# Ten more groups of spare products among the scores and state products of the first units, in a fused HGRN2 and FNet kernel

## The chip, the cores and the metric

The kernel runs on one core of one Trainium2 chip. The metric is device time in microseconds: 553.58, the median of 5 runs (553.43 to 553.75). TensorE (PE) multiplies and transposes, VectorE (DVE) and ScalarE (ACT) do the elementwise work, GpSimd (POOL) helps, and nearly all loads are issued from SyncE's queue (SP).

## What is computed

Two blocks follow each other. The first is a linear recurrence with a gate for each channel, over 4 batches, 8 heads, 768 tokens and 48 channels:

```python
f = 1.0 / (1.0 + np.exp(-f_logit))
for t in range(S):
    state = f[:, :, t, :, None] * state + np.einsum('bhd,bhe->bhde', k[:, :, t], v[:, :, t])
    y[:, :, t] = np.einsum('bhd,bhde->bhe', q[:, :, t], state)
```

The heads are then put side by side (384 columns), and the second block is an FNet mixer: u is x plus the real part of a two-dimensional FFT over tokens and columns; then u is normalized, multiplied by w_ch1 (384 x 1536), passed through a ReLU, multiplied by w_ch2 (1536 x 384) and added to u. Everything is in fp32; the weights arrive in double words and are converted in the kernel.

## The kernel before

**Units.** The recurrence is cut into 16 units of two heads of one batch (four units a batch). A unit is a Python generator, `attention`, that goes on in `outputs`; each call runs it to its next `yield`. Its steps, with the line numbers of the profile:

1. ACT: exp and ln of the gate (L330, L331).
2. DVE: the running sum of the gate's logarithm as a scan into W (L337), and chunk ends into `deep` (L338; POOL L339).
3. ACT: the exponentials (L342, L343, L345).
4. DVE: q and k are scaled in place (L349, L350).
5. PE: the **scores**, 24 small products in two halves (L361, `sc`).
6. DVE: the scores are masked into `at` (L368), one instruction for each half.
7. PE: five transposes of the scaled k (L506, `st`), and ACT copies them out (L508, `kT`).
8. PE: the **state products** k times v for each chunk (L517, `ds`).
9. DVE: the scan over chunk states (L525, `stt`).
10. PE: y within the chunks (L537).
11. PE: y from the earlier states, added to the same banks (L544); ACT: five copies to `yT` (L553 to L557).
12. PE: transposes of `yT` (L564, `yt`); ACT: copy into x (L566).
13. POOL and DVE: `fold`, sums and differences of x for the Fourier stage (L590 to L612).

The tiles `sc`, `st`, `ds` and `yt` share a PSUM pool of two buffers (`ps_a`), so each waits until the one before the last has been read.

**Behind the units.** For each batch `fnet` does the Fourier products (L650 `z`, L669 `mix`) and the normalization, whose rows are turned by PE (L708, `pt`). `projected` does the two big products (L750 `up`, L759 `po`, L773 `fx` and `fz`). Meanwhile the weights are converted block by block: ACT L238, DVE L240 and L241, POOL L242, each from one of three `raw` buffers.

**The order is written out by hand.** `ORDER` is one string of 676 words, and the loop at the end of the function runs one step for each word, in this order on every engine. A number is a step of that unit. L5qv loads q and v of unit 5 (f, k, q and v stand for the gate, k, q and v); r fetches a raw weight block and C converts one; F and H are steps of the Fourier stage, P of the projections. **D calls `busy` (L150)**:

```python
for _ in range(4):
    nc.tensor.matmul(spare, lhsT=bound[:, :C], rhs=bound[:, :2 * C], start=not started, stop=True,
                     skip_group_check=True)
    started.append(True)
```

A D is thus four products of 128 x 128 by 128 x 256 in bf16 on a constant tile, into 256 columns that nothing reads (L153). `spare` lies in the same PSUM tile as y, behind y's 768 columns, so a spare product can wait for ACT's copies of y. Before the change there are 21 such words, 84 products: 16 words in the first 13.7 us, three behind the scores of unit 3, and one behind the transposes of unit 4 and one before those of unit 5.

**Loads.** SP issues its DMAs in order, and each waits for the eighth before it. The load of a unit's q waits until PE has done L544 for the unit that used the same buffer (four buffers for q, three each for k and the gate).

Of the kernel before, what the change touches and what calls it, by code (L numbers as in the profile page):

```python
# [12 lines left out]
C = 128  # L13
# [12 lines left out]

ORDER = (
    "Gq2 r I D Gq0 L0f Gk1 L1f D Gk0 L0q i D Gq3 C Gq1 Z L0k 0 D 1 Gk2 0 L1q 1 L1k D D D D D D D D D D D "
    "D 0 0 1 0 r 1 L2f 0 2 C L1v 1 L3fk 1 3 L0v 0 1 L2q 2 0 0 r 1 L2k 3 1 0 2 r 3 L3q 2 L2v 0 C L3v C "
    "L4fk R 4 2 2 3 1 0 C 2 4 1 3 L5qv D L4qv L5fk 3 D D 3 2 0 2 3 2 3 C r 4 1 4 L6fk C r 2 5 4 L6qv 4 2 "  # L30
    "1 5 6 3 4 D 4 C 5 3 T 3 6 4 5 5 4 2 r L7fk 7 5 D L7qv 3 5 S L8fk C 4 7 6 6 5 F0 5 r r F0 F0 F0 7 4 "
    "C F0 L9fk 5 6 8 H0 H0 6 5 6 r H0 C L8qv 6 7 L9qv P0 6 7 r C P0 7 7 C 9 P0 r r 5 8 C r C F0 r 7 F0 6 "
    "P0 5 9 C 6 7 P0 r C P0 8 8 C P0 r r 7 P0 P0 8 9 H0 C P0 P0 8 7 8 C P0 H0 7 9 6 H0 H0 C 9 r C P0 9 "
    "L10fk r 9 P0 r C 9 L11fk 10 C 6 P0 11 4 P0 P0 P0 P0 P0 P0 10 P0 P0 P0 L10qv P0 P0 7 F1 9 P0 F1 H0 9 "
    "W P0 P0 P0 11 F1 P0 L11qv P0 P0 P0 9 P0 P0 P0 8 L12fk P0 11 11 8 P0 P0 10 11 F1 P0 11 11 10 L14fk "
    "F1 8 P0 14 F1 P0 10 P0 8 10 P0 P0 H1 H1 10 L12qv P0 P0 10 P0 F1 P0 11 11 10 P0 10 H1 P0 P0 P0 P0 12 "
    "12 12 P0 P0 12 P0 H1 P0 12 P0 H1 L13fk P1 P1 P1 P1 P1 14 13 P1 12 8 8 P1 P1 12 9 10 L13qv 13 P1 P1 "
    "L14qv 9 P1 12 11 P1 H1 11 10 P1 P1 13 P1 13 P1 12 P1 P1 14 P1 14 V 13 P1 c V 10 P1 P1 P1 P1 P1 V "
    "L15fk P1 13 P1 11 V P1 P1 P1 P1 c P1 11 F2 V c F2 F2 H1 13 H1 F2 c 14 P1 c V c P1 P1 12 P1 P1 14 P1 "
    "P1 13 V V V P1 15 F2 c P1 12 P1 P1 P1 P1 c P1 H2 14 15 V V P1 P1 P1 P1 P1 13 P1 14 F2 P1 c P1 P1 15 "  # L40
    "V 13 P1 H2 P1 P1 L15qv P1 14 13 P1 V 12 H2 F2 14 P2 P2 P2 P2 P2 P2 P2 15 P2 P2 P2 c c 12 H2 V H2 15 "
    "H2 15 P2 c P2 15 P2 P2 15 P2 14 13 15 P2 P2 14 P2 P2 15 13 P2 P2 P2 P2 P2 H2 V 15 P2 P2 14 15 H2 P2 "
    "P2 P2 P2 15 F3 F3 P2 F3 F3 P2 F3 c P2 P2 P2 P2 P2 V P2 c P2 V c c V P2 P2 P2 P2 P2 c P2 F3 F3 P2 V "
    "P2 H3 P2 P2 P2 H3 H3 P2 P2 P2 P2 P2 P2 P2 P2 P2 P2 P3 H3 c P3 P3 P3 P3 V P3 c P3 P3 P3 c V V c P3 "
    "P3 P3 H3 P3 P3 P3 P3 P3 P3 c P3 P3 V P3 H3 P3 P3 P3 P3 P3 P3 H3 H3 P3 P3 P3 P3 P3 P3 P3 P3 P3 P3 P3 "
    "P3 V P3 P3 P3 P3 P3 c P3 c P3 P3 P3 M P3 P3 P3 P3 P3 P3 P3 P3 P3 P3 P3 P3"
)

PAIRS = ((0, 3), (2, 5), (1, 4))
# [925 lines left out]
```

## Time and profile before

| | us |
|---|---|
| median of 5 runs | 553.58 (553.43 to 553.75) |
| the profiled execution | 554.17 |
| its span, from the first to the last instruction | 552.4 |
| PE busy | 525.4 (95%) |
| DVE busy | 299.7 (54%) |
| ACT busy | 192.6 (35%) |
| POOL busy | 94.4 (17%) |
| L153, the spare products | 84 of 0.27 each (median, pipelined) |

The profile is of one execution. Its rows are instructions with start and length, and consecutive ones of the same line are merged; `[1.34 <-DVE at L368]` says that the engine was idle for 1.34 us before the first of them and that DVE's L368 on tile `at` ended this. PEclk is the share of TensorE's clock that was granted. PE's products are pipelined: the length of one (0.27 us) is longer than the distance between two starts. A product in fp32 appears as two records.

### The profile page before, as it was taken

The numbers are of one execution on the slowest core, as the hardware profiler recorded it, in microseconds if no ns is written. First come the engines' busy times: TensorE is split into PE (matmuls) and PEld (weight loads), VectorE is DVE, ScalarE is ACT, GpSimd is POOL, SyncE is SP. The second block draws the span as 40 slices with busy tenths as digits, with TensorE's granted clock in tenths as the row PEclk, the third lists the DMA queues.
The fourth block names the chain that finished last, engine by engine and source line by source line (L and its number), as shares of the span: only waits on it lengthen the run. The fifth ranks groups of instructions, "written<-read, shape, count | busy, mean of one in ns | idle before, by whom it ended". The sixth has DMA issues, their size and how long they took to land.

```text
span 552.4 us, 10204 instructions
## 1 busy us (share of the span) xinstructions
PE 525.4 (95%) x4186; PEld 461.2 (83%) x4186; DVE 299.7 (54%) x534; ACT 192.6 (35%) x497; POOL 94.4 (17%) x147
## 2 busy tenths in 40 slices
PE   7787699999999999999999999999999999999995
PEld 5676578876898889889889899899889798989985
DVE  8899899984936527435744444453452342413231
ACT  5768286672332333441340422321411303021110
POOL 7146535534101000130201001003001000010000
PEclk9799799999999999999999999999999999999998
DMA  8989645463302100412530301102003004000001
GB/s 203 235 246 230 191 135 166 118 187 94 76 0 72 36 9 2 116 44 78 166 115 15 115 1 58 30 1 87 0 30 87 1 8 165 0 30 0 30 2 34
DMA packets 18398, 44.38 MB, mean 80 GB/s; under 512 B 3109, under 2 KB 4710, under 8 KB 18342
## 3 DMA queue, kind: packets, MB, share of 16 engines
q1 hardware_dynamic: 17094, 39.89, 26.6%
q0 software_dynamic: 1104, 3.54, 1.8%
q8 instruction: 35, 0.57, 0.5%
q10 hardware_dynamic: 144, 0.20, 0.1%
q14 instruction: 21, 0.17, 0.1%
HBM read 38.90 MB, written 4.72 MB: 79 GB/s over the span
## 4 chain that ended last, share of the span: by engine, by line
PE 86%; DMA 5%; ACT 3%; DVE 2%; POOL 1%; issue 1%; SPq 1%; ACTq 0%; POOLq 0%
PE up L750 34%; PE fx L773 16%; PE fz L773 12%; PE z L650 3%; PE y L537 3%; DMA g<-in_qkf_dram 3%; PE y L544 3%; PE sc L361 3%; PE po L759 3%; PE mix L669 3%; PE ds L517 2%; PE yt L564 1%; PE pt L708 1%; PE st L506 1%; DMA tab<-in_seq_tab_dram 1%; DMA q<-in_qkf_dram 1%
## 5 line engine op out<-in xcount | busy, mean ns | idle before, releaser
L750 PE MATMUL up<-unT,w 128*128 128x256 f32 x864 | 197.0, 382 | 1.5 <-DVE x L728 0.9
L750 PEld LDWEIGHTS up<-unT,w 128*128 128x128 f32 x864 | 161.0, 190 | 26.1 <-issue 1.5
L752 ACT ACTIVATE h<-up 128x256 f32<-128x256 f32 x144 | 55.2, 383 | 199.2 <-PE up L750 199.2
L617 POOL DMA_INDIRECT out_dram<-x,place x16 | 16.9, 1057 | 270.7 <-DVE x L803 232.6
L773 PE MATMUL fx<-block,h 128*128 128x192 f32 x264 | 46.5, 326 | 0.0
L773 PE MATMUL fx<-w,h 128*128 128x192 f32 x264 | 44.9, 327 | 0.1
L773 PEld LDWEIGHTS fx<-w,h 128*128 128x128 f32 x264 | 43.1, 190 | 0.8 <-ACT h L752 0.4
L773 PEld LDWEIGHTS fx<-block,h 128*128 128x128 f32 x264 | 43.5, 190 | 0.0
L242 POOL TENSOR_TENSOR w<-w,raw 128x384 uint32<-128x384 uint32 x24 | 29.7, 1244 | 47.8 <-ACT raw L238 24.0
L780 DVE TENSOR_TENSOR s<-h,h 128x768 f32<-128x768 f32 x11 | 10.5, 954 | 50.4 <-ACT h L752 50.4
L361 PE MATMUL sc<-q,W 48*64 48x128 f32 x768 | 26.4, 283 | 7.4 <-issue 4.4
L361 PEld LDWEIGHTS sc<-q,W 48*64 48x64 f32 x768 | 22.0, 138 | 11.6 <-issue 6.9
L368 DVE COPY_PREDICATED at<-causal,sc 128x768 f32<-128x768 uint32 x32 | 31.2, 1032 | 0.8 <-PE sc L361 0.8
L337 DVE TENSOR_TENSOR_SCAN W<-g,bound 112x768 f32<-112x768 f32 x16 | 29.5, 1843 | 1.0 <-issue 0.5
L725 DVE TENSOR_TENSOR x<-mix,x 128x384 f32<-128x384 f32 x12 | 6.6, 553 | 38.6 <-PE mix L669 38.6
L537 PE MATMUL y<-at,v 128*64 128x128 f32 (+1 forms) x384 | 26.2, 287 | 0.0
L537 PEld LDWEIGHTS y<-at,v 128*64 128x64 f32 (+1 forms) x384 | 22.6, 137 | 3.1 <-issue 2.9
L773 PE MATMUL fz<-w,s 128*128 128x192 f32 x132 | 23.5, 328 | 0.0
L773 PE MATMUL fz<-block,h 128*128 128x192 f32 x132 | 23.5, 328 | 0.0
L773 PE MATMUL fz<-w,h 128*128 128x192 f32 x132 | 23.4, 327 | 0.0
L695 ACT ACTIVATE rstd<-mv,eps 128x1 f32<-128x1 f32 (+1 forms) x20 | 5.9, 294 | 46.0 <-DVE mv L692 46.0
L773 PEld LDWEIGHTS fz<-w,s 128*128 128x128 f32 x132 | 21.6, 190 | 0.3 <-issue 0.3
(145 smaller groups left out, 743.3 us busy)
## 6 DMA issues: line engine op xcount, KB each, us to landing
raw<-in_w_ch_dram SPq DMA_DIRECT2D x24, 384.0 KB, 4.8
g<-in_qkf_dram SPq DMA_DIRECT2D x32, 144.0 KB, 4.6
q<-in_qkf_dram SPq DMA_DIRECT2D x32, 144.0 KB, 4.6
k<-in_qkf_dram SPq DMA_DIRECT2D x32, 144.0 KB, 5.4
v<-in_v_dram SPq DMA_DIRECT2D x16, 288.0 KB, 4.9
k<-in_w_ch_dram SPq DMA_DIRECT2D x12, 384.0 KB, 4.0
g<-in_w_ch_dram SPq DMA_DIRECT2D x12, 384.0 KB, 4.3
out_dram<-x SPq DMA_DIRECT2D x4, 168.0 KB, 2.1
```

Source lines behind the costliest of these rows:

```text
L242: nc.gpsimd.tensor_tensor(bits, bits, lo, ALU.add)
L337: nc.vector.tensor_tensor_scan(W, g, bound[:R], 0.0, ALU.add, ALU.min)
L361: nc.tensor.matmul(ps[64 * s:64 * s + 64, r, i * C:(i + 1) * C], lhsT=W[ROWS[r], o + 64 * s:o + 64 * s + 64], rhs=Q[ROWS[r], o:o + C], sta ...
L368: nc.vector.copy_predicated(AT[:, :, half], causal.bitcast(U32).unsqueeze(1).unsqueeze(1).to_broadcast([128, 2, NCH // 2, C]), ps[:, :, :N ...
L537: nc.tensor.matmul(y[FILL[r], c * C:(c + 1) * C], lhsT=vt[:, c, r * D:r * D + (64 if r == 0 else D)], rhs=AT[:, r, c], start=(c % 4 == 0), ...
L544: nc.tensor.matmul(y[ROWS[r], c * C:(c + 1) * C], lhsT=st[ROWS[r], :, c - 1], rhs=Q[ROWS[r], c * C:(c + 1) * C], start=False, stop=True, s ...
L617: nc.gpsimd.indirect_dma_start(out=out.rearrange("b s d -> (b s) d"), out_offset=bass.IndirectOffsetOnAxis(ap=place[:, b, i:i + 1], axis=0 ...
L650: nc.tensor.matmul(z[:, cols], lhsT=src[:, j, lo:hi], rhs=tab[:, t, T % 2, cols], start=(i == 0), stop=(i == len(parts) - 1), skip_group_c ...
L669: nc.tensor.matmul(mix[:, o], lhsT=zz[:rows_of[T], T, PLACES[c]], rhs=cd[:rows_of[T], T, :NQ - odd], start=(i == 0), stop=(i == 1))
L750: nc.tensor.matmul(pp[:, :256], lhsT=w1[:, kt, m * 128:(m + 1) * 128], rhs=unT[:, kt], start=(kt == 0), stop=(kt == 2))
L752: nc.scalar.activation(hs[-1][:, m % H].rearrange("p t n -> p (t n)"), pp[:, :256], AF.Relu)
L773: nc.tensor.matmul(out, lhsT=h[:, m], rhs=blocks[i][:, m], start=(start and m == 0), stop=(m == H - 1), skip_group_check=True)
```

## The change

Ten more words D stand in `ORDER`, in four places; nothing else differs. The words around them, with the new ones as `+D`:

```
D 0 0 1 0 +D +D +D r 1 L2f 0 2 C L1v 1 +D +D L3fk 1 3 L0v 0 1
L5qv D L4qv L5fk 3 D D +D +D +D 3 2 0 2 3 2 3 C r 4 1 +D +D 4 L6fk C r 2 5 4
```

On PE the 40 new products come to stand

- (a) 12 between the scores of unit 0 and the scores of unit 1,
- (b) 8 between the scores of unit 1 and the transposes of unit 0,
- (c) 12 behind the scores of unit 3 and the 12 spares that stand there already, ahead of the transposes of unit 3,
- (d) 8 between the transposes of `yT` of unit 1 and L544 of unit 2.

The core of the diff (the string is wrapped anew behind each place):

```diff
-    "D 0 0 1 0 r 1 L2f 0 2 C L1v 1 L3fk 1 3 L0v 0 1 L2q 2 0 0 r 1 L2k 3 1 0 2 r 3 L3q 2 L2v 0 C L3v C "
-    "L4fk R 4 2 2 3 1 0 C 2 4 1 3 L5qv D L4qv L5fk 3 D D 3 2 0 2 3 2 3 C r 4 1 4 L6fk C r 2 5 4 L6qv 4 2 "
+    "D 0 0 1 0 D D D r 1 L2f 0 2 C L1v 1 D D L3fk 1 3 L0v 0 1 L2q 2 0 0 r 1 L2k 3 1 0 2 r 3 L3q 2 L2v 0 "
+    "C L3v C L4fk R 4 2 2 3 1 0 C 2 4 1 3 L5qv D L4qv L5fk 3 D D D D D 3 2 0 2 3 2 3 C r 4 1 D D 4 L6fk "
```

## Prediction

> **What bounds the kernel now.** I read the page's slices first, then the busy times on a grid of short stretches, then the timelines of TensorE (PE) and VectorE (DVE) around the four places.
>
> ```profile
> PE   7787699999999999999999999999999999999995
> DVE  8899899984936527435744444453452342413231
> PEclk9799799999999999999999999999999999999998
> ```
>
> From the seventh slice on (13.8 us each) PE is full, and in 85 to 548 us it is busy for 459.29 of 463.00 us. Whatever is gained or lost before about 85 us is carried unchanged to the end. Before that PE has gaps, DVE is the full engine, and the granted clock dips twice.
>
> The clock moves on a grid. One-microsecond stretches give a mean clock of 0.74 in 19:20 and 0.85 in 26:27, so it was halved from 19.48 to 26.30 us; 0.51 in 57:58 and 0.58 in 63:64 give 57.02 to 63.84. These are steps of 6.82, 30.72 and 6.82 us, all multiples of 3.41. So I asked for stretches of that length (start:end, length, busy us and instructions of PE, PEld, DVE, ACT, POOL, then the clock):
>
> ```profile
> 16.06:19.48 3.42, 1.79 (x49) 1.30 (x49) 3.39 (x6) 2.93 (x6) 0.88 (x1) 1.00 1.02 218
> 19.48:22.89 3.41, 2.63 (x21) 2.22 (x23) 2.79 (x3) 2.42 (x6) 0.33 (x2) 0.50 1.07 252
> 22.89:26.30 3.41, 3.41 (x52) 3.41 (x50) 2.43 (x3) 2.04 (x3) 0.00 (x0) 0.50 1.03 242
> 43.37:46.78 3.41, 1.94 (x52) 1.75 (x54) 3.29 (x4) 3.29 (x10) 1.61 (x1) 1.00 1.02 242
> 53.61:57.02 3.41, 1.09 (x12) 0.66 (x8) 3.38 (x4) 2.52 (x8) 1.94 (x5) 1.00 0.80 209
> ```
>
> The clock fell after PE was busy for 1.79 and 1.09 us, and did not fall after 1.94 us. The sign of a fall is a stretch about half empty.
>
> ```profile
> 16.76 1.81 PE L361 MATMUL sc<-q,W 48*64 48x128 f32 x48 [1.34 <-DVE at L368]
> 19.46 2.13 PE L506 MATMUL st<-ident,W 112*128 112x112 f32 x10 [0.89 <-DVE at L368]
> 22.38 2.42 PE L517 MATMUL ds<-v,kT 128*64 128x48 f32 x39 [0.78 <-ACT kT L508]
> ```
>
> This is PE in the first dip. The state products (ds) took 2.42 us; the same 39 at full clock take 1.40 (at 39.69, below).
>
> **Parts (a) and (b): 12 spares between the scores of units 0 and 1, 8 between the scores of unit 1 and the transposes of unit 0.** A spare costs 0.109 us on PE: twelve took 1.47 us from first start to last end with a pipeline tail of 0.27 (the row at 36.99 below), so (1.47-0.27)/11. Twelve cost 1.31 and eight 0.87 at full clock, about double at half clock (an estimate from the 2.42 against 1.40 of ds, which is 1.7). The scores of unit 0 issue until 15.26 (13.88+1.54-0.27+0.11) and those of unit 1 wait until 16.76 for DVE's L368: 1.31 fits into that 1.50. The scores of unit 1 issue until 18.41 and the transposes wait until 19.46, again for L368: 0.87 fits into 1.05. So both cost nothing while L368 is late; if that cover were gone they would cost 2.18.
>
> What they buy: stretch 16.06:19.48 rises from 1.79 busy to about 1.79+0.5+0.87 = 3.1, far above the 1.94 that kept its clock. So the fall at 19.48 goes. The transposes then end earlier, but ds starts at 22.38 as before, since its v arrives only then (SP's queue records the landing of that v at 22.24). With ds at full clock its first half ends after 0.85 (row at 68.19, x20) instead of some 1.4, so DVE's state scan, 23.84 before, starts about 0.54 earlier. This carries to the scores of unit 2 (28.94, right after DVE's L350).
>
> **Is it kept?** Not on DVE:
>
> ```profile
> 34.31 0.36 DVE L240 TENSOR_SCALAR w<-raw 128x384 uint32<-128x384 uint32 x1 [0.16 <-DMA raw<-in_w_ch_dram]
> ...
> 40.47 0.36 DVE L593 TENSOR_TENSOR eo<-eo 128x192 f32<-128x192 f32 x1
> 40.74 1.40 DVE L525 TENSOR_TENSOR_SCAN stt<-ds,te 112x288 f32<-112x288 f32 x2
> 42.06 0.34 DVE L240 TENSOR_SCALAR w<-raw 128x384 uint32<-128x384 uint32 x1
> 42.44 0.84 DVE L241 SCALAR_TENSOR_TENSOR w<-raw,w 128x384 uint32<-128x384 uint32 x1
> ```
>
> At 34.31 DVE waits for a weight block that was issued at 28.40 from a stream that fills the DMA engines (share about 1.0 from 5 to 34 us), so arriving 0.54 earlier only lengthens that wait. From 34.31 on DVE is busy back to back up to the second `pt` transposes, apart from 1.49 us at 60.49 that wait for POOL, which itself waits for DVE:
>
> ```profile
> 80.77 0.52 PE L708 MATMUL pt<-ident,un 128*128 128x128 f32 x3 [0.17 <-PE sc L361]
> ...
> 83.57 0.55 PE L708 MATMUL pt<-ident,un 128*128 128x128 f32 x3 [0.38 <-DVE un L705]
> ```
>
> PE waits for DVE at 83.57 and hardly again. So the time is what DVE's chain from 34.31 to 83.51 makes it. Parts (a) and (b): 0 (bounds -0.54 and 0).
>
> **Part (c): 12 more spares behind the 12 already there, ahead of the transposes of unit 3.**
>
> ```profile
> 36.99 1.47 PE L153 MATMUL y<-bound 128*128 128x256 bf16 x12
> 38.77 0.70 PE L506 MATMUL st<-ident,W 112*128 112x112 f32 x5 [0.31 <-DVE at L368]
> 39.69 1.40 PE L517 MATMUL ds<-v,kT 128*64 128x48 f32 x39 [0.22 <-DVE at L368]
> ```
>
> Here the cover is 0.31 us and the new work 1.31. The last of 24 spares starts at 36.99+23x0.109 = 39.50, the transposes at 39.61 instead of 38.77 (+0.84). They end at 40.31, and the kT copy on ACT (0.63, at 39.50 before) ends at 40.97. The ds of unit 2 follow the transposes at 40.13, end at 40.98, and DVE's first scan starts at 41.02 instead of 40.74 (+0.28, since L593 ends at 40.83). The ds of unit 3 wait for kT, run 41.02 to 41.87, and the second scan starts at 41.90 instead of 41.41: **+0.49 on DVE**, the engine without slack. Part comes back: L241 at 42.44 took 0.84 against 0.56 at 34.71, while POOL's L596 ran until 42.86; 0.49 later it starts after that and takes 0.56. That leaves **+0.21**. Behind it POOL's L242 (1.61 at 43.41) and DVE's L350 (1.76 against 0.95 at 33.19) obstruct each other as before, both 0.21 later. Bounds: 0 if ds is quicker, +0.49 if nothing comes back.
>
> **Part (d): 8 spares ahead of the inter-chunk products of unit 2 (L544, 43.13).** +0.87 and the delay of (c) put their end near 46.0 instead of 44.47. PE was then idle until 45.94, when the scores of unit 4 wait for DVE's L350, itself 0.21 later: hidden, with about 0.2 to spare. ACT's copies of y2 move from 44.51 to 46.0; ACT was idle from 47.27 to 48.87 before. SP's q load for unit 6 waits for L544 and goes from 45.49 to about 46.0; the load behind it starts at 47.26. Cost 0; without this cover up to 0.87.
>
> The order of instructions on DVE, ACT, POOL and SP does not change. **Sum:** 0 + 0 + 0.21 + 0 = +0.21 us. The profiled execution took 554.17 us around its span of 552.4; the median of the five runs is 553.58. I apply the difference to the median: 553.8.
>
> The Trainium skill, page "TensorE: Matmul & The Clock Gate", Part 1, says that the clock halves after at least one idle window of about 3.4 us on a free-running grid. The row 16.06:19.48 agrees in the length but not in "idle": PE was busy for 1.79 of 3.42 us. By the page's wording nothing would fall there and (a) and (b) would buy nothing; by the row they buy 0.54, which DVE then loses. Either way the sum is +0.21. The page's free-running grid speaks against spares at fixed places, since another execution could have other windows; no run here shows that, and five runs lie within 0.32 us.
>
> **Rivals.**
> 1. *The clock falls later instead (slower).* With ds and y0 at full clock, PE reaches the end of unit 0's L544 at about 26.5 instead of 28.25, and still waits for DVE until 28.40. Stretch 26.30:29.72, 2.74 busy before, would hold about 0.2 + 1.3 = 1.5, less than the 1.79 that fell. Then 29.72:33.13 runs at half clock and loses 1.71; unit 1's L544 ends at 33.93+1.71 = 35.64 instead of 34.49, and with it the q load on SP. The chain of waits runs from exactly there (SP, q, g, table, g until 65.8, ACT, z at 72.22): +1.15, 554.7; with a second half-clock stretch +2.86, 556.4. It decides when that stretch is emptier than about 1.8. For: the numbers above. Against: stretch 19.48:22.89 (about 1.9 busy with everything at full clock) may fall first, as a rest of the old dip up to 26.30; then the change barely does what it says, and the time is my forecast's.
> 2. *The DMA chain binds, not DVE.* The chain of waits goes from L544 at 34.49 through SP and DMA; 0.54 earlier there gives 553.0. For: the page's chain. Against: DVE without gaps beside it.
> 3. *DVE and POOL fall differently.* The scan at 52.69 took 3.24 against 1.75 elsewhere while POOL did 1.5 us of work; this can vanish (-1.49+0.21, 552.3) or arise at another scan, such as 49.95 (+1.7, 555.3).
>
> **Chances.** Forecast, 553.4 to 554.1: 0.55. Rival 1: 0.16, of which 0.12 is slower by over 0.2% (1.1 us, about what a measurement of this kernel can tell from no change). Rival 2: 0.14. Rival 3: 0.15, of which 0.08 faster and 0.07 slower. So faster 0.08, same 0.73, slower 0.19. The range 552.6 to 554.9 takes in the bounds of (a) to (d), rival 2 and rival 1's first price; it leaves out rival 3's ends and rival 1's second price.
>
> **What the new profile would show.** Right: clock 1.00 in 19.48:22.89; the waits before the transposes at 19.46 unchanged; DVE still waiting at 34.3; the ds of unit 3 and the second scan near 41.9; `pt` at 83.8. Rival 1: a clock of 0.50 in 29.72:33.13. I am wrong if DVE's wait at 34.31 goes, if scans change by over 1 us, or if PE at 83.57 no longer waits for DVE.

## The result: slower by 0.32%

The changed kernel took **555.93 us** (median of 42 executions) against 554.14 for the kernel before (median of 73 on the same chips): a ratio of **1.0032, interval 1.0022 to 1.0042**, or 1.8 us (1.2 to 2.3). Two executions of the changed kernel, at 690.6 and 691.2 us with a mean granted clock of 0.75, were disturbed and are left out of the ratio. The prediction was 553.8 with a range of 552.6 to 554.9, and 0.73 for "within 0.2%": wrong. The kernel before also shows that five executions had been too few: 73 of them lie between 552.7 and 557.9.

### The profile page after: what moved, and what is told of

It is laid out like the page before. It is cut to its first block, busy times and chain, and to the rows that moved or that the text cites. A ratio compares the mean times of both kernels' runs of the same rounds, so it can differ in the third digit from the quotient of the medians.

```text
span 552.8 us, 10284 instructions
## 1 busy us (share of the span) xinstructions
PE 527.8 (95%) x4226; PEld 463.5 (84%) x4226; DVE 299.4 (54%) x534; ACT 192.5 (35%) x497; POOL 94.5 (17%) x147
## 3 DMA queue, kind: packets, MB, share of 16 engines
q0 software_dynamic: 1104, 3.54, 1.9%
## 4 chain that ended last, share of the span: by engine, by line
PE 85%; DMA 6%; ACT 3%; DVE 3%; issue 1%; POOL 1%; SPq 0%; ACTq 0%; DVEq 0%; POOLq 0%
PE up L750 34%; PE fx L773 15%; PE fz L773 12%; PE z L650 3%; PE y L537 3%; PE sc L361 3%; PE po L759 3%; PE mix L669 3%; PE y L544 3%; DMA raw<-in_w_ch_dram 2%; DMA g<-in_qkf_dram 2%; PE ds L517 2%; PE yt L564 1%; PE pt L708 1%; DMA tab<-in_seq_tab_dram 1%; PE st L506 1%
## 5 line engine op out<-in xcount | busy, mean ns | idle before, releaser
L617 POOL DMA_INDIRECT out_dram<-x,place x16 | 16.9, 1057 | 270.2 <-DVE x L803 234.6
L368 DVE COPY_PREDICATED at<-causal,sc 128x768 f32<-128x768 uint32 x32 | 31.2, 1029 | 0.8 <-PE sc L361 0.8
L361 PE MATMUL sc<-q,W 48*64 48x128 f32 x768 | 26.5, 284 | 5.0 <-issue 4.2
L361 PEld LDWEIGHTS sc<-q,W 48*64 48x64 f32 x768 | 22.2, 138 | 8.7 <-issue 6.3
L773 PEld LDWEIGHTS fz<-block,h 128*128 128x128 f32 x132 | 21.6, 190 | 0.3
```

Source lines behind the costliest of these rows:

```text
L361: nc.tensor.matmul(ps[64 * s:64 * s + 64, r, i * C:(i + 1) * C], lhsT=W[ROWS[r], o + 64 * s:o + 64 * s + 64], rhs=Q[ROWS[r], o:o + C], sta ...
L368: nc.vector.copy_predicated(AT[:, :, half], causal.bitcast(U32).unsqueeze(1).unsqueeze(1).to_broadcast([128, 2, NCH // 2, C]), ps[:, :, :N ...
L617: nc.gpsimd.indirect_dma_start(out=out.rearrange("b s d -> (b s) d"), out_offset=bass.IndirectOffsetOnAxis(ap=place[:, b, i:i + 1], axis=0 ...
L773: nc.tensor.matmul(out, lhsT=h[:, m], rhs=blocks[i][:, m], start=(start and m == 0), stop=(m == H - 1), skip_group_check=True)
```

## The profile after

The profiled execution took 554.56 us around a span of 552.8. From the page, the slices of PE, DVE and PEclk:

```profile
PE   6897699999999999999999999999999999999995
DVE  8999899984936437427644345344452441413231
PEclk9989799999999999999999999999999999999999
```

PE's first seven slices read 6 8 9 7 6 9 9 instead of 7 7 8 7 6 9 9, and the rest of its row is the same. The timeline of PE around (a) to (c) (start, length, group, and what ended the idle time before it):

```profile
16.27 1.82 PE L361 MATMUL sc<-q,W 48*64 48x128 f32 x48
18.02 1.05 PE L153 MATMUL y<-bound 128*128 128x256 bf16 x8
18.99 0.70 PE L506 MATMUL st<-ident,W 112*128 112x112 f32 x5
...
20.55 1.55 PE L517 MATMUL ds<-v,kT 128*64 128x48 f32 x39
...
26.74 1.73 PE L361 MATMUL sc<-q,W 48*64 48x128 f32 x48 [1.99 <-issue]
28.40 2.82 PE L537 MATMUL y<-at,v 128*64 128x128 f32 x24
...
35.02 2.79 PE L153 MATMUL y<-bound 128*128 128x256 bf16 x24
37.66 0.64 PE L506 MATMUL st<-ident,W 112*128 112x112 f32 x5
38.23 1.55 PE L517 MATMUL ds<-v,kT 128*64 128x48 f32 x39
```

The waits for L368 at 16.76 and 19.46 are gone, filled with spares. The 39 `ds` start at 20.55, 1.83 us earlier than before, and take 1.55 us instead of 2.42. But the 24 `y` products at 28.40 take 2.82, nearly twice the 1.52 that they take at full clock (e1's row below). The stretches of the clock's grid in this execution (start:end, length, busy us of PE, PEld, DVE, ACT, POOL, then the clock) say why:

```profile
17.72:21.14 3.42, 3.19 (x53) 2.40 (x44) 3.42 (x4) 2.06 (x5) 1.02 (x1) 1.00 1.05 263
21.14:24.55 3.41, 3.41 (x70) 3.10 (x66) 3.34 (x6) 2.48 (x5) 0.38 (x2) 1.00 1.03 252
24.55:27.96 3.41, 1.42 (x48) 1.25 (x48) 3.34 (x7) 3.32 (x10) 0.00 (x0) 1.00 1.06 268
27.96:31.38 3.42, 3.42 (x37) 2.76 (x30) 3.42 (x5) 1.68 (x4) 2.20 (x2) 0.50 0.99 229
```

This is rival 1's mechanism: the fall has moved behind the emptied stretch at 24.55 (1.42 busy of 3.41). But rival 1's price does not show here. At the transposes that the prediction used as its meeting point, PE is **earlier** than before:

```profile
79.79 0.52 PE L708 MATMUL pt<-ident,un 128*128 128x128 f32 x3 [0.17 <-PE sc L361]
...
82.59 0.55 PE L708 MATMUL pt<-ident,un 128*128 128x128 f32 x3 [0.39 <-DVE un L705]
```

82.59 against 83.57 before: 0.98 us earlier, and no loss. (That the change brought these 0.98 is not shown: e3, e5 and e9 below lack (a) and (b) and are 1.2 to 1.8 us earlier too, so the profile before was of a late execution here.) So the loss lies behind 85 us, where the prediction had PE full. Matching each product of PE with the same product before, the 0.98 stays constant up to one place. Before:

```profile
342.48 1.52 PE L537 MATMUL y<-at,v 128*64 128x128 f32 x24
344.34 3.94 PE L750 MATMUL up<-unT,w 128*128 128x256 f32 x17 [0.33 <-ACT unT L709]
```

After:

```profile
341.49 1.52 PE L537 MATMUL y<-at,v 128*64 128x128 f32 x24
344.32 3.94 PE L750 MATMUL up<-unT,w 128*128 128x256 f32 x17 [1.30 <-ACT unT L709]
```

PE arrives 0.99 earlier and waits 0.97 longer. Followed backwards on ACT's timeline: L709 stands behind L566 (the copy of `yt` into x), and that copy now waits for a DMA. Before:

```profile
343.26 0.64 ACT L566 COPY x<-yt 128x576 f32<-128x576 f32 x1 [1.99 <-DVE x L725]
```

After:

```profile
343.25 0.64 ACT L566 COPY x<-yt 128x576 f32<-128x576 f32 x1 [2.96 <-DMA out_dram<-x]
```

The copy writes into a buffer of x whose rows are still being stored to `out`. In the trace the last of three stores from SP lands at 343.09 before and 343.07 after, each 0.17 to 0.18 ahead of the copy, and so it is in every profile of this study where the landing is recorded: the store sets the copy in both, whatever the row names. SP's three stores (L624) stand behind POOL's indirect store (L617, issued at 337.64 before, 336.65 after). The DMA view of 336 to 342 us shows that store's time to landing, before:

```profile
out_dram<-x,place POOLq DMA_INDIRECT x1, 2.6
```

After, with a line of the queue list that is not there before:

```profile
q8 instruction: 1, 0.02, 1.2%
...
out_dram<-x,place POOLq DMA_INDIRECT x1, 3.5
```

Queue q8, of the kind instruction, moves one packet of 16 KB at a time, 35 in the run; that they are blocks of PE's program is read from their moving with its length, below. In the packed records one of them begins at 337.8 after; before, the nearest begin at 326.8 and 345.7. The 40 new products are 80 more records of PE and PEld, and make all later fetches come earlier. So this is the explanation to be tested, **theory 3** below: the length of PE's program puts a fetch on the stores that PE waits for.

The Trainium skill, "Runtime: NRT & Kernel Launch", section "Instruction fetch mechanics", says that programs are refilled in blocks of 16 KiB, 256 instructions, by a DMA queue of the sequencer's own, and calls the cost mostly hidden. The blocks agree (8372 records of PE and PEld, that is rows of the trace, in 35 packets before: 239 each). Hidden it is for PE itself, which shows no wait for it, but not for the store beside it: 3.54 us instead of 2.58.

## Experiments

Each kernel was compared with the kernel before on the same chip, in 12 executions where a ratio is given. Theory 1: (c) and (d) cost. Theory 2: (a) and (b) move the clock's fall, and this costs. Theory 3: above; in the expectations of e1 to e4 it is still the plainer "each spare costs the same wherever it stands", and from e5 on it is the place of a fetch. "The wait" is PE's wait for `unT` at 344. Line numbers shift by 2 to 13 where the edit adds lines.

**e1, e2, e3: parts alone.** `ORDER` with the words of (a)+(b), of (c)+(d), of (c).

> Only the five words of places (a) and (b): 20 spares between the scores of units 0 and 1 and ahead of the transposes of unit 0. Theory 1 (cover: the cost is PE work ahead of the transposes of unit 3 and of L544 of unit 2, that is (c) and (d)): ratio 1.000, within 0.001. Theory 2 (clock: (a) and (b) lift the fall at 19.5 us, the clock falls in the next empty stretch instead, and this costs): the whole loss, 1.003. Theory 3 (each spare costs the same wherever it stands, as through fetching a longer PE program): half, 1.0015.

> Only the five words of places (c) and (d): 20 spares ahead of the transposes of unit 3 and ahead of L544 of unit 2. Theory 1 (cover): the whole loss, 1.003. Theory 2 (clock): 1.000, and the first dip of the clock as before. Theory 3 (each spare costs the same): 1.0015.

> Only the three words of place (c), ahead of the transposes of unit 3. Theory 1 with my prediction's term for (c), +0.2 to +0.5 us: 1.0004 to 1.0009, the rest of the loss then belongs to (d); if (c) alone carries it, 1.003. Theory 2: 1.000. Theory 3: 0.3 of the loss, 1.001.

Measured: (a)+(b) 1.0042 (1.0017 to 1.0067), (c)+(d) 1.0012 (0.9996 to 1.0028), (c) 0.9999 (0.9982 to 1.0016). So (c) alone costs nothing that can be measured, and theory 1 fails: by it (a)+(b) should have cost nothing. By the ratios alone theory 2 did best, since it expected 1.003, 1.000 and 1.000. But e1's ratio comes from seven long executions of 557.5 to 559.3 us; the other five, 553.2 to 555.6, are no slower than the kernel before on that chip (554.94). So e1's 0.42% can't be read as the price of the fetch. PE's wait at 344 is 1.56, 1.39 and 0.33. In e1 and e2 (40 records more) POOL's store takes its 2.6; there SP's issue of the third store is slow, 1.61 and 1.43 instead of 0.38, and both measured SP stores land late. e1, DMA view of 336 to 342 us:

```profile
q8 instruction: 1, 0.02, 1.2%
...
out_dram<-x SPq DMA_DIRECT2D x1, 168.0 KB, 3.4
out_dram<-x SPq DMA_DIRECT2D x1, 22.5 KB, 2.7
out_dram<-x,place POOLq DMA_INDIRECT x1, 2.6
```

Before, the two took 2.1 and 1.5. In e3 (24 records) the fetch comes at 341.3, after all three issues.

**e4: all ten words again.** No edit; to see whether the loss at 344 repeats.

> The changed kernel once more, for a second profile of it and for the spread. All theories: 1.0032 within 0.001. What the profile may add: my prediction took one execution's windows for all; theory 2 expects the clock to fall in another stretch in this profile than in the first one (there 27.96 to 31.38).

Measured: 1.0028 (1.0005 to 1.0051); wait 1.24, the indirect store 3.5. The clock fell elsewhere, as expected: from 26.94 to 33.77, two stretches.

**e5: only the length.** The kernel before, each of the first 40 spares (all before 14 us) in two halves: the same columns, 80 records more.

```diff
         for _ in range(4):
-            nc.tensor.matmul(spare, lhsT=bound[:, :C], rhs=bound[:, :2 * C], start=not started, stop=True,
-                             skip_group_check=True)
+            for o in ((0, C) if len(started) < 40 else (0,)):
+                n = C if len(started) < 40 else 2 * C
+                nc.tensor.matmul(spare[:, o:o + n], lhsT=bound[:, :C], rhs=bound[:, :n], start=not started and o == 0,
+                                 stop=True, skip_group_check=True)
             started.append(True)
```

> The kernel before without any new spare; its first 40 spares are written as 80 products of half the columns, so that PE's program is 80 records longer, as in the changed kernel, while the columns that PE streams stay the same. Theory 3 (length of the PE program: it moves the fetch of a 16 KB block of instructions, which in the changed kernel falls at 337.8 us beside the store that PE waits for at 344): PE's wait for ACT's unT near 344 us is 1.2 to 1.6 us instead of 0.33, ratio 1.0015 to 1.002. Theory 2 (the clock after (a) and (b)): wait 0.33, ratio 1.000.

Measured: 1.0028 (1.0008 to 1.0048), without one new spare beyond 14 us; the expected 1.0015 to 1.002 lies inside the interval. Its DMA view and its PE timeline repeat what the change showed:

```profile
q8 instruction: 1, 0.02, 1.0%
...
out_dram<-x,place POOLq DMA_INDIRECT x1, 3.5
```

```profile
344.01 4.15 PE L752 MATMUL up<-unT,w 128*128 128x256 f32 x18 [1.22 <-ACT unT L711]
```

**e6, e7: the words without the length.** All ten words with the first 80 spares merged in pairs to 40 products of 512 columns; (a)+(b) with the first 40 merged to 20. PE's program is as long as before. The edit of e6 (e7 has 40 for 80):

```diff
-            nc.tensor.matmul(spare, lhsT=bound[:, :C], rhs=bound[:, :2 * C], start=not started, stop=True,
-                             skip_group_check=True)
+            wide_one = len(started) < 80
+            if not (wide_one and len(started) % 2):
+                nc.tensor.matmul(both[:, 4 * C:8 * C] if wide_one else spare, lhsT=bound[:, :C],
+                                 rhs=bound[:, :4 * C if wide_one else 2 * C], start=not started, stop=True,
+                                 skip_group_check=True)
```

> All ten new words, with the first 80 of the 124 spares written as 40 products of twice the columns: the same columns at the same places as in the changed kernel, and a PE program of the length of before. Theory 3: the wait near 344 us is back at 0.33, and the ratio falls from 1.003 to 1.001 or below. Theory 2: the ratio stays at 1.003, whatever the wait at 344 us does.

> Places (a) and (b) alone, with the first 40 spares written as 20 products of twice the columns, so that the program has the length of before. Theory 3: the 1.0042 of (a) and (b) alone falls to 1.001 or below. Theory 2: it stays near 1.004.

Measured: 1.0016 (0.9998 to 1.0033) and 0.9997 (0.9977 to 1.0018); waits 0.33 and 0.32. So the wait goes with the length, with the words in place. Of the loss of all ten words about half goes; 1.0016 is above the expected 1.001. The loss of (a)+(b) is gone too, but with it the group of long executions (e7's highest is 555.8), which no profile here explains.

**e9, e10: a longer program.** If length costs by itself, more of it costs more; if the place of the fetch counts, 160 records more should put it ahead of the stores. e9 is the kernel before with its first 40 spares in three parts; e10 has all ten words and e5's halves.

```diff
+            parts = ((0, 88), (88, 84), (172, 84)) if len(started) < 40 else ((0, 2 * C),)
+            for o, n in parts:
...
```

> The kernel before with each of its first 40 spares cut into three products (88, 84 and 84 columns): the same columns, 160 records of PE more, all in the first 14 us. Theory 3 (the length of the program of PE, by the place of an instruction fetch): a fetch comes about every 256 records; 80 records more moved the one at 345.7 us to 337.6, among the stores of x at 336 to 341, and PE then waited 1.2 us at 344. With 160 it should fall near 332, ahead of these stores: PE's wait for ACT's unT near 344 is 0.3 again, and the ratio is 1.000 (up to 1.001). Rival (each record more costs time of its own, wherever the fetch falls): twice the loss of 80 records, a ratio near 1.005.

> All ten new words, and in addition the first 40 spares cut into halves, so that PE's program is 160 records longer than before instead of 80. Theory 3: the wait near 344 falls from 1.3 to 0.3 us and the kernel is quicker than the changed one although its program is longer: a ratio to the kernel before of about 1.001 (what the merged form with the ten words kept), not 1.003. Rival (each record costs): 1.005 or more.

Measured: 1.0017 (0.9998 to 1.0036) and **1.0006 (0.9986 to 1.0025)**; the fetch begins at 330.6 and 332.4. e10 runs the ten words and 80 records more than the changed kernel, and its median is 554.88 (554.21 for the kernel before on the same chip) against 555.93 (554.14). Its PE timeline:

```profile
344.38 3.94 PE L752 MATMUL up<-unT,w 128*128 128x256 f32 x17 [0.33 <-ACT unT L711]
```

e9's ratio is above the 1.001 expected, though far from the rival's 1.005; its wait is 0.35.

**e8, e11, e12, e15 to e17: (a)+(b) once more each; e18: all ten words once more.** One profile each, to catch the longest executions: in e1 seven of twelve took 557.5 to 559.3, of the changed kernel ten of forty 557.8 to 559.7.

> Places (a) and (b) alone once more, for another profile. Of the twelve times of its first run seven lie at 557.5 to 559.3 us and five at 553.2 to 555.6, and the profile kept is of a short one (553.96). Theory 2: a profile of a long execution shows two or three more stretches at half clock before 85 us and PE at the second pt transposes 3 to 4 us later. Theory 3: the additional time sits behind 85 us, at PE's waits for stores or loads.

> Parts (a) and (b) alone once more, for a profile of one of its long executions (7 of 12 took 557.5 to 559.3 us, 5 took 553.2 to 555.6, and both profiles so far are of short ones). Theory 3: in a long one the extra 4 us stand at the stores near 340 and in the wait near 344. Theory 2 (clock): they stand before 85 us, in a clock that is halved for longer there. If it is a short one: 554, with a wait of 1.3 to 1.6 near 344.

> The same kernel a second time in this call, with the same expectation: a long execution (558) shows where its extra 4 us stand (near 344 by theory 3, before 85 us by theory 2); a short one (554) shows a wait of 1.3 to 1.6 near 344.

> Parts (a) and (b) alone, one more profile, to catch an execution of 557.5 us or more. If the instruction fetch is behind the long group, PE's wait near 344 is 3 us or more in it, or a second wait of that kind stands elsewhere behind 85 us; from the start of the first pt products to the end it takes more than 475.1 us. If it is the early part, pt starts at 82.5 or later and the rest takes 474.5 to 475.1 as in the other profiles of this kernel.

> The same, once more: pt at 82.5 or later with 474.5 to 475.1 behind it (early part), or more than 475.1 behind it (fetch or another wait).

> The same, once more: pt at 82.5 or later with 474.5 to 475.1 behind it (early part), or more than 475.1 behind it (fetch or another wait).

> The changed kernel, once more: behind pt 474.5 to 475.1 with a wait of 1.2 to 1.3 near 344; an execution of 557.5 or more has pt at 82.5 or later (early part), or more than 475.1 behind it.

Measured: 553.89, 556.27, 556.84, 554.52, 554.35, 555.10 and 554.51: none of the long group. e18's wait, 1.69, is longer than the expected 1.2 to 1.3. What sets the long group **stays open**. In e11 and e12, the longest, the extra stands before 85 us (pt at 81.51 and 81.75, 79.07 in e1), and the clock fell in rival 1's stretch. e11's stretches:

```profile
24.55:27.96 3.41, 1.47 (x46) 1.28 (x46) 3.38 (x6) 3.32 (x9) 0.01 (x1) 1.00 1.04 263
27.96:31.38 3.42, 3.42 (x47) 3.03 (x38) 3.38 (x6) 1.02 (x3) 2.21 (x2) 0.50 1.04 242
```

and the same `y` products in e11 and, at full clock, in e1:

```profile
28.90 2.71 PE L537 MATMUL y<-at,v 128*64 128x128 f32 x24
```

```profile
28.30 1.52 PE L537 MATMUL y<-at,v 128*64 128x128 f32 x24
```

**e13, e14: is the clock worth anything?** e13: (a)+(b), and 12 spares more in PE's wait ahead of the scores of unit 2, 25.06 to 27.0 in e11 (in a bank of the Fourier pool), at the length of before. e14: the same with (d), and 8 and 20 more in the waits before L564 at 55.59 and before L361 at 59.37 (places in the profile before), at the length of e9.

```diff
+            elif kind == "E":
+                busy_apart()
...
+        for _ in range(4):
+            nc.tensor.matmul(apart[0][:, :2 * C], lhsT=bound[:, :C], rhs=bound[:, :2 * C], start=True, stop=True,
+                             skip_group_check=True)
```

> Parts (a) and (b), and twelve more spares between L544 of unit 0 and the scores of unit 2, where PE waits 1.94 us for DVE (they write a bank of the Fourier stage's pool, which nothing uses yet, so they wait for nobody); the first 64 spares merged to 32 of 512 columns, so that PE's program has the length of before. Theory 2 (clock): in the profiles of (a)+(b) the clock fell at 28 us where a stretch of the grid ended between 26.9 and 28.6 (busy 1.5 of 3.41 us or less), and not where it ended at 29 or at 26.6; a fall cost 2.3 to 2.8 us. Filled, no stretch there holds less than 2.5, so no execution falls at 28: a ratio of 0.997 (0.995 to 0.999), and none of the executions above 556.5. Theory 3 alone (length): as with the merged form of (a)+(b), 0.9997, with the same spread of 4 us.

> The same filling, the merged spares undone, part (d) and not (c), and 8 and 20 spares more in PE's two waits at 53.9 (1.69 us) and 56.4 (2.97 us), ahead of the second fall of the clock; 12 of the first spares cut into halves, so that PE's program is 160 records longer than before, the length at which the wait near 344 was 0.3. Theory 2: the clock stays at 1.00 from about 9 to 548 us whatever the grid; products between 57 and 64 us run at full speed; DVE binds most of that stretch, so that I estimate 0 to 1.5 us more than the run before: a ratio of 0.994 to 0.998. If the spares delay PE where DVE waits for it, 1.000 or above.

Measured: **1.0004 (0.9986 to 1.0021)** and **1.0009 (0.9992 to 1.0026)**: neither brought the gain that theory 2 expected. It fails as an account of the median. The clock did what was meant, e14 from 39.70 on:

```profile
36.28:39.70 3.42, 3.42 (x21) 2.55 (x21) 3.28 (x6) 0.06 (x1) 1.38 (x3) 0.50 1.05 252
39.70:72.00 32.30, 26.38 (x397) 21.68 (x397) 28.42 (x47) 21.10 (x49) 17.84 (x33) 1.00 0.73 188
```

and PE then stands idle longer ahead of pt, 1.11 us for DVE where it was 0.17 in all, and pt starts at 80.50 against 80.77 before:

```profile
80.50 0.52 PE L720 MATMUL pt<-ident,un 128*128 128x128 f32 x3 [1.11 <-DVE un L717]
```

No kernel here beats the one before: the two lowest ratios, 0.9997 and 0.9999, have intervals on both sides of 1.

**All twenty profiles in one table.** The fetch's start relative to POOL's store, PE's wait at 344, the start of the first pt, and the execution's time behind that start (us, computed from the traces):

```
          fetch-store  wait   pt     behind pt
before       +8.0      0.33  80.77   473.40
e3           +5.3      0.33  79.16   473.92
e6           +7.9      0.33  79.25   473.76
e7           +7.9      0.32  78.59   473.96
e13          +7.8      0.33  80.70   473.61
e9           -5.3      0.35  79.02   473.42
e10          -5.3      0.33  80.83   473.41
e14          -5.3      0.33  80.50   473.52
after        +1.1      1.30  79.79   474.77
e4           +1.1      1.24  81.06   474.67
e5           +1.2      1.22  79.55   474.49
e18          +1.2      1.69  79.56   474.95
e1           +3.4      1.56  79.07   474.89
e2           +3.4      1.39  82.27   474.78
e8           +3.4      1.31  79.23   474.66
e11          +3.4      1.39  81.51   474.76
e12          +3.3      1.70  81.75   475.09
e15          +3.3      1.30  80.08   474.44
e16          +3.3      1.62  79.28   475.07
e17          +3.4      1.40  80.57   474.53
```

With a fetch 1.1 to 3.4 us behind the store the last column is 474.44 to 475.09 (mean 474.76), with any other place 473.40 to 473.96 (mean 473.63). The groups don't touch; **1.13 us** lie between them. The first pt varies by 3.7 us, and by 2.7 within (a)+(b), the same program each time. The ratios split in the same way, though with some overlap: 1.0012 to 1.0042 where the fetch falls on the stores (after, e1, e2, e4, e5; mean 1.0028, of which e1's long executions are a part), 0.9997 to 1.0017 elsewhere (e3, e6, e7, e9, e10, e13, e14; mean 1.0007).

Two more workings from the same traces bind the loss to the fetch. Matched product by product with the profile before, PE loses 0.85 to 1.36 us (mean 1.07) at the `up` products of 344, and at no other place behind pt, in each of the twelve profiles with the fetch beside the stores; in the other seven it loses nothing there (under 0.1 us from pt to the last product). And the hold-up is about as long as the fetch's packet, within 0.15 us in all twelve:

```
            packet of the fetch   POOL's store beyond 2.58
e5                0.98                  0.88
e4                1.05                  0.91
after             1.11                  0.96
e18               1.43                  1.36
                                  SP's third issue beyond 0.38
e2                0.96                  1.05
e8                0.96                  0.97
e11               0.96                  1.05
e17               0.96                  1.05
e15               1.01                  0.96
e1                1.15                  1.23
e16               1.29                  1.28
e12               1.36                  1.38
```

So it is shown that a fetch beside the stores makes them late by about its own length, and PE with them, for five lengths of program (0, 24, 40, 80 and 160 records more), with and without new words. By which part of the DMA path a fetch holds up POOL's store in one case and SP's issue in the other, the traces don't tell.

## Why the prediction was wrong, step by step

- **"Whatever is gained or lost before about 85 us is carried unchanged to the end": this step failed.** The 0.98 us by which the profiled execution was ahead at pt were lost at one wait, at 344 us. PE's 459.29 busy of 463.00 us was read as "no wait behind here can change". But the 0.33 us at 344 hung, with nothing to spare, on a DMA store that the change could delay.
- **The sum counted the new products as time on PE only.** Their 80 records in PE's program were no term of it. That term is 1.13 us by the table. Of the measured 1.8 (1.2 to 2.3) it leaves 0.6 (0.1 to 1.2), against +0.21 predicted. Where the words stand without the collision, e6 and e10 give 0.9 and 0.3 us (1.0016 and 1.0006), neither apart from zero. Ten of the forty executions behind the ratio belong to the long group; the other thirty have a median of 555.42, 1.28 above the kernel before. So most of the rest may be what the long group adds, an estimate made after the fact. What sets that group, and so the rest, stays open.
- **(a) and (b) cost nothing: right.** Scores of unit 1 and transposes came 2.89 and 5.61 us behind the first scores (13.38 in this profile), against 2.88 and 5.58 before (13.88), and e7 is at 0.9997.
- **"The fall at 19.48 goes ... buying 0.54 that DVE loses at 34.31": the right end by reasons that hold for one execution.** That `ds` starts at 22.38 because its v comes then was true of the profile before alone: it starts between 20.53 and 21.82 in all the others but e2 (23.89), with and without the words. In the changed profile DVE reaches its raw block 2.3 us earlier (32.02) and hardly waits, because the block is there earlier too (landed at 31.99, 34.29 before). The prediction named the end of this wait as a sign of being wrong; it came, but is not what cost the time. The grid of the clock differs in every execution, so a sum made on one execution's stretches was no sum for the median.
- **(c), +0.49 on DVE and 0.28 back: the mechanism is seen in the trace, the size was not general.** In the changed profile DVE waits for the late `ds`, and L241 takes 0.56 instead of 0.84:

```profile
39.13 1.54 DVE L525 TENSOR_TENSOR_SCAN stt<-ds,te 112x288 f32<-112x288 f32 x2 [0.60 <-PE ds L517]
40.59 0.34 DVE L240 TENSOR_SCALAR w<-raw 128x384 uint32<-128x384 uint32 x1
40.96 0.56 DVE L241 SCALAR_TENSOR_TENSOR w<-raw,w 128x384 uint32<-128x384 uint32 x1
```

  From the start of L593 to that of L240 DVE took 1.59 us before, 2.01 in e3, where (c) stands alone, and 2.42 in the changed profile. So the +0.49 is +0.42 and +0.83, and with the 0.28 back the net is about +0.14 and +0.55 in place of +0.21. All of these are too small for e3's interval (-1.0 to +0.9 us).
- **(d) hidden: not refuted.** In the changed profile the scores of unit 4 start 0.11 us behind the end of DVE's L350, as before. e2 cost 0.66 us, and its own profile has 1.06 more of the wait at 344.
- **Rival 1: the mechanism was right, its price is not shown.** The fall came behind the emptied stretch, at 27.96, but the changed profile had lost nothing by pt. In (a)+(b), pt starts at 81.51, 81.75 and 80.08 with the fall at 28 and at 79.07, 79.23, 79.28 and 80.57 without it, 1.6 us apart in the mean but with overlap; with all ten words, 79.79, 79.56 and 79.25 with it, 81.06 where it lasted two stretches (e4), and 80.83 without (e10). So a price of about the 1.15 that the rival named is neither shown nor excluded for single executions; filling the stretch (e13) moved no median.

## What to carry to other kernels

A product that hides in a wait still lengthens its engine's program, and so, as here on PE, moves every later instruction fetch. Before calling a tail "carried unchanged", list the waits in it that hang on a DMA, however short, and ask what lands beside that DMA. When the change is well under the spread between executions, test length and work apart: the same columns in more products, and the new work at the old length.

## What the runs showed of the hardware

- A 16 KB instruction fetch (one packet of 0.96 to 1.43 us) beside a store lengthened an indirect store from 2.58 to 3.5 us (up to 3.94 in e18), or the issue of a store on SP from 0.38 to between 1.3 and 1.8 us.
- The clock's first rise lay at 6.94 to 9.89 us in the profiles, and every later change a multiple of 3.41 behind it. The Trainium skill, "TensorE: Matmul & The Clock Gate", Part 1, calls this grid free-running; the profiles here agree, which one profile could not show. It lets the clock halve after an idle window. Here stretches with PE busy for 1.42 of 3.41 us were enough, and one with 2.16 (32.87 to 36.28 in e14), while 1.94 in the profile before was not: busy time alone does not decide it.
- Keeping the clock at full from 39.7 to 548 us (e14) was worth nothing that could be measured (1.0009, 0.9992 to 1.0026); ahead of pt PE stood idle for 1.11 us, until DVE was done, against 0.17 before.
